# One of each head's sums of kept scores and negated maximum made by an accumulating DMA

## The chip, the cores and the metric

The kernel runs on one core of a Trainium2 chip. The core has TensorE (PE, with its weight loads as PEld), VectorE (DVE), ScalarE (ACT), GpSimd (POOL) and SyncE (SP). Each engine works through its own queue in the order in which the program was written, and waits at an instruction until the semaphores it names have come. Transfers run on 16 DMA engines that all queues share. The metric is the device time of one execution in microseconds (us). Three runs of the kernel before took 1121.7, 1123.69 and 1124.69 us; the median is 1123.69 us.

## The reference, cut to what matters

The input x has 2048 rows of 448 values in fp32. It is normalised, and one block of attention (16 heads of 28 columns that share one key and one value) and one gated MLP with 1792 hidden columns both read the result. Their sum with x is the output.

```
xn = layernorm(x)
q = (xn @ wq) as 16 heads of 28;  k = xn @ wk;  v = xn @ wv      # k and v shared by all heads
p = softmax(q @ k.T * 28 ** -0.5)                                 # exact maximum taken out per query row
att = (p @ v, heads side by side) @ wo
h = silu(xn @ w1) * (xn @ w3)
out = x + att + h @ w2
```

## The kernel before, in words

The 2048 query rows are cut into four chunks of 512. A head in the sense of the kernel is one of the 16 heads on one chunk, so there are 64, numbered 0 to 63. For each of them the 2048 keys are 16 tiles of 128. Scores stand transposed: a tile has 128 keys in its partitions and 512 queries along them.

Each head passes through two stages. In the first, `leads`, PE makes all 16 score tiles (`ld`, 16 matmuls of 512 columns) and DVE takes a running maximum of them (`mx`, L800 and L803). Ten or twelve of the 16 tiles are kept: ACT copies them from PSUM into SBUF (`pa`, L797), two tiles to a pair of 128 x 1024. The column maxima are folded, negated and stored in DRAM as one row of 512 values (`md`). Two transfers read that row back: one appends it to the queries (`qs`), one spreads it over 128 partitions (`mb`, 256 KB).

In the second stage, `weights_of`, a kept pair has the negated maximum added by POOL (L839: `pa` plus `mb`, 128 x 1024) and goes through the exponential in place on ACT (L841). The tiles that were not kept are computed again by PE with the maximum as an 85th row (`sc`, L846), and ACT takes their exponential from PSUM (`pb`, L849). In `values`, PE multiplies eight tiles by v (`av`, L866), four of this head and four of the head before it. Two heads that run at once fill the time between them: a head begins every half `T`.

The keeping plan is `TEN` (pairs that begin at tiles 2, 5, 8, 11, 14) or, for every second head from head 12, `TWELVE` (1, 4, 6, 9, 11, 14): 346 pairs in all. The last pair of a head in the order of the second stage is always the one that begins at tile 14.

Beside this the MLP runs as 56 steps (14 hidden tiles for each chunk): gate `g` and up `u` matmuls, tanh on ACT, two products on DVE, a high and a low part `h` on ACT and POOL (L698, L700), then the down products `dn`. In the first chunk, weights are read raw, split into a high and a low part by ACT and POOL (L650, L652, L666, L668) and stored in DRAM; later chunks load them from there.

The order of the work is made by a planner inside the kernel. Every instruction gets an engine, a cost and a due time. The planner then plays the machine through and lets each free engine take, of the work whose inputs are ready and whose buffers are free, the piece that is due first. Buffers are pages of 2 KB a partition and pairs of them; `MOST`, `SPARE`, `SOON` and `EARLY` limit who may hold how many. `PUT` shifts the due time of each kind of work. `T0`, `T`, `LEAD`, `SPAN`, `XDUE`, `MDUE` and the like set the due times of heads and of MLP steps, and `RATE`, `LATE` and `BACKLOG` describe transfers. So a change of a table reorders all five queues.

Of the kernel before, what the change touches and what calls it, by code (L numbers as in the profile page):

```python
# [13 lines left out]
ALU = mybir.AluOpType  # L14
# [6 lines left out]
P = 128  # L21
TC = 512
# [21 lines left out]
AVK = 4  # L44
T0, T, LEAD, SPAN = 73.28, 32.63, 14.04, 29.75
XDUE = (4.15, 8.15, 12.15, 16.15)
QDUE, QSTEP = 21.57, 6.09
SINGLE = 2
XSTORE = 22.5, 16.1
MDUE, MRUSH, MSTEP = 40, 11, 10.34  # L50
MEND = 7.58
RATE = 18.1
QUEUES = 16
LANES = 8
BACKLOG = 1565.91
LATE = 901.2
HLV = 0
EARLY = 16
BULK = ("w13", "w2", "x", "raw", "raw2", "acc")
SOON = {"pa": 30.2, "qs": 15.3, "acc": 15.9, "o": 18.3, "x": 24.2}  # L60

PUT = {"ACT ": -1.32, "ACT at pa": 0.93, "ACT at pb": -0.15, "ACT at x": 1.75, "ACT at xp": 8.68,
        "ACT av o": -9.5, "ACT h mi": -0.39, "ACT h t": -0.01, "ACT kv qp": -3.95, "ACT lb o oh": -0.08,
        "ACT mi t": -0.59, "ACT mi x": 2.0, "ACT o oh": 1.81, "ACT qp qt": -0.15, "ACT raw w13": -16.73,
        "ACT raw wo": 7.09, "DVE ": 1.37, "DVE acc": -5.45, "DVE acc xn": -2.36, "DVE at m": -0.89,
# [11 lines left out]
PAIRS = 39  # L77
PAGES = 96 - 2 * PAIRS
SLACK = 5.49
REST = 70.26  # L80
LOADING = 60
BANKS = 8
MOST = {"pa": 33, "x": 25, "acc": 10, "w13": 9, "w2": 8, "h": 3, "oh": 12, "wo": 4, "xt": 3, "xn": 1, "wq": 14,
        "qt": 4, "pb": 12, "raw": 4, "raw2": 5, "t": 2, "qs": 5, "m": 4, "mxt": 7, "mb": 7, "o": 19, "lb": 7,
        "xp": 33, "wr": 8, "kv": 7, "at": 5, "mi": 21, "av": 9, "qp": 14}
SPARE = {"x": 2, "acc": 4, "w13": 2, "w2": 4, "raw": 2, "raw2": 2, "qt": 6, "wo": 1, "qs": 2}

# [26 lines left out]
class Plan:  # L114
# [42 lines left out]
    def order(self):  # L157
# [8 lines left out]
        queues, landed = [0.0] * QUEUES, [0.0] * LANES  # L166
# [50 lines left out]
        now, todo = 0.0, len(self.ops)  # L217
        while todo:
            progress = True
            while progress:  # L220
                progress = False
                for e in self.ENGINES:
# [16 lines left out]
                    o = best  # L239
# [9 lines left out]
                    if o.port:  # L249
# [95 lines left out]
def build(ctx, tc, x, wq, wk, wv, wo, w1, w3, w2, out):  # L345
    nc = tc.nc
    plan = Plan()
# [21 lines left out]
    def fixed(ap):  # L369
        return Buf(None, "fixed", ap=ap)  # L370
# [11 lines left out]
    def gps(n, fn, **k):  # L382
        return plan.op("POOL", pool(n), fn, lat=pool_lat(n), **k)
# [67 lines left out]
    acc = {}  # L451
# [24 lines left out]
    for g, (lo, hi) in enumerate(QROWS):  # L476
        b = page("wr", f"wqr{g}")
# [22 lines left out]
    for qc in range(NQ):  # L500
# [3 lines left out]
        for t in range(TT):  # L504
            sbf = fixed(sts[t])
            b, m = x_in[qc][t], mvb[qc][t]
# [250 lines left out]
    stacks, pt, mbs, avb, og, ohl = {}, {}, {}, {}, {}, {}  # L757
    lead_first, av_last = {}, [None]
    md = {h: dr.tile([1, TC], F32, tag=f"md{h}", name=f"md{h}") for h in range(NH)}
# [3 lines left out]
    def kept(h):  # L763
        return TWELVE if h >= FROM and h % OF < MANY else TEN

    def begin(h):
# [12 lines left out]
    def leads(h):  # L779
# [51 lines left out]
    def weights_of(h, i):  # L831
# [5 lines left out]
        if kt in keeps:  # L837
            p, b = pt[h, kt][0], mbs[h]
            gps(1024, lambda: nc.gpsimd.tensor_add(p.ap, p.ap, b.ap.unsqueeze(1).broadcast_to([P, 2, TC])),  # L839
                reads=[b], writes=[p], prio=-3.0)  # L840
            act(1024, lambda: nc.scalar.activation(p.ap, p.ap, AF.Exp, scale=SCALE), psum=False, writes=[p],  # L841
# [175 lines left out]
```

## Time and profile before

| | value |
|---|---|
| three runs, us | 1121.7, 1123.69, 1124.69 |
| the profiled execution: span from first to last instruction, us | 1120.7 |
| what the runs lie above that span, us | 1.0 to 4.0, the median 3.0 |
| busy of the span: PE, POOL, ACT, DVE | 99%, 89%, 88%, 84% |
| 346 kept pairs on POOL, mean ns and sum | 2412 ns, 821.7 us |
| DMA: share of 16 engines, moved | 46.9%, 167.50 MB |

The profile's span runs from the first instruction to the last; the time of a run also holds what lies around them. Of the profiled execution the page has the span alone. Busy time of an engine says how much of the span it worked; the table of stretches says when. An engine that idles costs something only if another one, which sets the end, waits for it. A row of a wait names the waiting instruction first and then what released it.

### The profile page before, as it was taken

Reading aid. Unit: us, or ns where it says so; the run is one execution under the profiler, and the core shown is the slowest. Engines: PE = TensorE matmul, PEld = TensorE weight load, DVE = VectorE, ACT = ScalarE, POOL = GpSimd, SP = SyncE. Lnnn points to the kernel's source line nnn. Section 1 sums busy time; section 2 is a strip of 40 time slices with the busy share of each in tenths; the row PEclk is TensorE's granted clock in tenths of the full one; section 3 lists DMA queues with packets and bytes.
Section 4 is the critical chain, followed back from the end, with each engine's and each line's share of the span. In section 5 each row is a group of like instructions: output and inputs, shape, how many; then the busy total and the mean of one; then the engine's idle time right before and its main releaser. Section 6 shows DMA issues by size and latency. Waiting matters only on the chain.

```text
span 1120.7 us, 18422 instructions
## 1 busy us (share of the span) xinstructions
PE 1104.6 (99%) x5758; PEld 736.5 (66%) x5758; DVE 946.0 (84%) x1802; ACT 982.9 (88%) x1628; POOL 994.1 (89%) x499
## 2 busy tenths in 40 slices
PE   6999999999999999999999999999999999999998
PEld 4877667666666676666666666666666676667664
DVE  7879776898898989899899888899889889898834
ACT  3466888999999989999899999999899989998962
POOL 3226999999999998999999998999989999999983
PEclk9999999999999999999999999999999999999999
DMA  6887777576425246242631461514452534335410
GB/s 180 264 264 257 254 255 255 159 227 214 164 62 155 69 135 207 59 140 75 232 124 50 148 224 53 166 45 156 142 173 75 174 127 150 102 92 161 142 56 33
DMA packets 99017, 168.66 MB, mean 150 GB/s; under 512 B 19804, under 2 KB 61468, under 8 KB 98920
## 3 DMA queue, kind: packets, MB, share of 16 engines
q1 hardware_dynamic: 98920, 167.50, 46.9%
q8 instruction: 45, 0.74, 0.3%
q14 instruction: 52, 0.43, 0.1%
HBM read 126.94 MB, written 39.83 MB: 149 GB/s over the span
## 4 chain that ended last, share of the span: by engine, by line
PE 94%; DVE 2%; ACT 2%; DMA 1%; issue 0%; SPq 0%; DVEq 0%; ACTq 0%
PE ld L792 22%; PE av L866 21%; PE g L409 12%; PE u L409 12%; PE dn L409 11%; PE sc L846 8%; PE q L409 4%; PE wo L409 3%; PE xp L541 1%; DVE mx L803 1%; ACT pa L841 1%; ACT pa L797 1%; DVE acc L723 1%; DMA acc<-x 0%; DVE sums L939 0%
## 5 line engine op out<-in xcount | busy, mean ns | idle before, releaser
L839 POOL TENSOR_TENSOR pa<-pa,mb 128x1024 f32<-128x1024 f32 x346 | 821.7, 2412 | 9.0 <-DMA mb<-md 6.4
L803 DVE TENSOR_TENSOR mx<-ld,mx 128x512 f32<-128x512 f32 x896 | 581.9, 682 | 73.0 <-PE ld L792 49.1
L797 ACT ACTIVATE pa<-ld 128x512 f32<-128x512 f32 x692 | 400.8, 622 | 39.7 <-PE ld L792 30.3
L841 ACT ACTIVATE pa<-pa 128x1024 f32<-128x1024 f32 x346 | 373.9, 1088 | 14.8 <-POOL pa L839 14.3
L792 PE MATMUL ld<-qs,kst 84*128 84x512 f32 x1024 | 351.4, 405 | 0.4 <-DVE mx L803 0.2
L792 PEld LDWEIGHTS ld<-qs,kst 84*128 84x128 f32 x1024 | 189.9, 189 | 100.8 <-DVE mx L803 21.6
L866 PE MATMUL av<-pa,vst 128*32 128x512 f32 x1384 | 248.3, 599 | 0.0
L866 PE MATMUL av<-pb,vst 128*32 128x512 f32 x664 | 245.6, 597 | 0.0
L849 ACT ACTIVATE pb<-sc 128x512 f32<-128x512 f32 x332 | 202.6, 617 | 17.3 <-PE sc L846 16.5
L409 PE MATMUL dn<-w,h 128*128 128x448 f32 x672 | 156.7, 368 | 0.0
L409 PEld LDWEIGHTS dn<-w,h 128*128 128x128 f32 x672 | 125.6, 188 | 23.3 <-issue 3.0
L846 PE MATMUL sc<-qs,kst 85*128 85x512 f32 x332 | 134.7, 410 | 0.0
L866 PEld LDWEIGHTS av<-pa,vst 128*32 128x32 f32 x1384 | 51.6, 109 | 91.7 <-issue 82.9
L700 POOL TENSOR_TENSOR h<-t,h 128x512 fp32r<-128x512 f32 x56 | 72.7, 1299 | 41.9 <-ACT h L698 40.6
L846 PEld LDWEIGHTS sc<-qs,kst 85*128 85x128 f32 x332 | 62.6, 188 | 45.7 <-DVE mx L803 11.1
L652 POOL TENSOR_TENSOR w<-raw,w 128x512 fp32r<-128x512 f32 x28 | 36.2, 1302 | 42.7 <-ACT w L650 25.2
L866 PEld LDWEIGHTS av<-pb,vst 128*32 128x32 f32 x664 | 48.1, 109 | 33.2 <-issue 33.2
L723 DVE TENSOR_TENSOR acc<-dn,acc 128x448 f32<-128x448 f32 x80 | 49.4, 618 | 23.0 <-PE dn L409 21.9
L409 PE MATMUL g<-x_0m,w 128*128 128x512 f32 x168 | 58.1, 396 | 0.0
L409 PE MATMUL g<-x_2m,w 128*128 128x512 f32 x168 | 56.6, 396 | 0.0
L409 PE MATMUL u<-x_2m,w 128*128 128x512 f32 x168 | 54.9, 393 | 0.0
L409 PE MATMUL u<-x_0m,w 128*128 128x512 f32 x168 | 54.9, 395 | 0.0
(85 smaller groups left out, 1187.0 us busy)
## 6 DMA issues: line engine op xcount, KB each, us to landing
w<-w13s SPq DMA_DIRECT2D x84, 512.0 KB
w<-w2s SPq DMA_DIRECT2D x42, 448.0 KB
mb<-md SPq DMA_DIRECT2D x64, 256.0 KB
w13s<-w SPq DMA_DIRECT2D x28, 512.0 KB
qs<-qd SPq DMA_DIRECT2D x64, 112.0 KB
wo<-wos SPq DMA_DIRECT2D x16, 448.0 KB
w2s<-w SPq DMA_DIRECT2D x14, 448.0 KB
raw<-w SPq DMA_DIRECT2D x28, 192.0 KB
```

Source lines behind the costliest of these rows:

```text
L409: nc.tensor.matmul(dst.ap[0:n, 0:width], lv(lb), rv(rb), start=(i == 0), stop=(i == len(terms) - 1))
L652: gps(512, lambda: nc.gpsimd.tensor_sub(l.ap, r.ap, f32(h.ap)), reads=[r, h], writes=[l], prio=-6.0)
L700: sub(512, lambda: eng.tensor_sub(hl.ap, p.ap, f32(hh.ap)), reads=[p, hh], writes=[hl], prio=2 * half)
L723: vec(448, lambda: nc.vector.tensor_add(a.ap[:, 0:D], o.ap[:, 0:D], a.ap[:, 0:D]), reads=[o, a], prio=1.0))
L792: last = pe(512, lambda m=m, kt=kt: nc.tensor.matmul(m.ap, kst_ap[0:KS, kt * P:(kt + 1) * P], q.ap[0:KS], start=True, stop=True), reads=[q ...
L797: act(512, lambda m=m, p=p, i=int(kt not in keeps): nc.scalar.activation(p.ap[:, i], m.ap, AF.Copy), reads=[m], parts=[p])
L803: vec(512, lambda m=m: nc.vector.tensor_max(mx.ap, m.ap, mx.ap), reads=[m], writes=[mx])
L839: gps(1024, lambda: nc.gpsimd.tensor_add(p.ap, p.ap, b.ap.unsqueeze(1).broadcast_to([P, 2, TC])), reads=[b], writes=[p], prio=-3.0)
L841: act(1024, lambda: nc.scalar.activation(p.ap, p.ap, AF.Exp, scale=SCALE), psum=False, writes=[p], prio=-1.0, after=[sqrt_last])
L846: pe(512, lambda: nc.tensor.matmul(o.ap, kst_ap[0:KS + 1, kt * P:(kt + 1) * P], q.ap[0:KS + 1], start=True, stop=True), reads=[q, kst[kt / ...
L849: act(512, lambda: nc.scalar.activation(p.ap, o.ap, AF.Exp, scale=SCALE), reads=[o], writes=[p], prio=0.0, after=[sqrt_last])
L866: nc.tensor.matmul(a.ap[r:r + 32], vst_ap[:, kept(g)[2][n]], p.ap if i is None else p.ap[:, i], start=(n < 2), stop=(n >= KT - 2), skip_gr ...
```

## The change

For each head one kept pair, the one that begins at tile 14, no longer gets its negated maximum from POOL's add. POOL issues a DMA instead (L850 after the change) that reads the row `md` from DRAM, repeated for 128 partitions and both tiles, and adds it to the pair in SBUF. The other four or five pairs of the head are added by POOL as before (L854), with `mb`, which is still loaded. So 64 of the 346 adds become 64 DMAs, and the exponential of these pairs waits for the DMA. `BYDMA` is the number of such pairs per head, `ISSUE` the time in ns that the planner books on POOL for one, `AHEAD` the shift of its due time in us. The planner also learns that a transfer can come from POOL.

The DMA scratch in SBUF is set to 4096 bytes a partition, and the planner's buffers grow from 96 to 102 pages of 2 KB, three of which pairs more: 42 instead of 39. All tables of the planner are given new numbers.

```
-T0, T, LEAD, SPAN = 73.28, 32.63, 14.04, 29.75
+BYDMA, ISSUE, AHEAD = 1, 1000.0, -18.18
+T0, T, LEAD, SPAN = 71.07, 32.62, 14.04, 29.77
...
-MDUE, MRUSH, MSTEP = 40, 11, 10.34
-MEND = 7.58
+MDUE, MRUSH, MSTEP = 39.93, 11, 11.03
+MEND = 9.81
...
-PAIRS = 39
-PAGES = 96 - 2 * PAIRS
+PAIRS = 42
+PAGES = 102 - 2 * PAIRS
...
-                    if e == "SP":
+                    if o.size:
+                        begun = now if e == "SP" else now + o.cost
                         for j in range(o.k):
-                            queues[j] = max(queues[j], now) + o.size / o.k / RATE
+                            queues[j] = max(queues[j], begun) + o.size / o.k / RATE
...
+    def n_of(keeps, order, kt):
+
+        return [k for k in order if k in keeps].index(kt)
...
-        d = fixed(md[h])
+        d = mdb[h] = fixed(md[h])
...
         if kt in keeps:
             p, b = pt[h, kt][0], mbs[h]
-            gps(1024, lambda: nc.gpsimd.tensor_add(p.ap, p.ap, b.ap.unsqueeze(1).broadcast_to([P, 2, TC])),
-                reads=[b], writes=[p], prio=-3.0)
+            if n_of(keeps, order, kt) >= len(keeps) - BYDMA:
+                plan.op("POOL", ISSUE, lambda: nc.gpsimd.dma_start(
+                    p.ap, md[h].unsqueeze(1).broadcast_to([P, 2, TC]), accum_op=ALU.add),
+                    reads=[mdb[h]], writes=[p], prio=AHEAD, size=2 * 2 * P * TC * 4)
+            else:
+                gps(1024, lambda: nc.gpsimd.tensor_add(p.ap, p.ap, b.ap.unsqueeze(1).broadcast_to([P, 2, TC])),
+                    reads=[b], writes=[p], prio=-3.0)
             act(1024, lambda: nc.scalar.activation(p.ap, p.ap, AF.Exp, scale=SCALE), psum=False, writes=[p],
                 prio=-1.0, after=[sqrt_last])
...
-    nc = _bacc.Bacc("TRN2", target_bir_lowering=False, num_devices=1)
+    nc = _bacc.Bacc("TRN2", target_bir_lowering=False, num_devices=1, dynamic_dma_scratch_size=4096)
```

Three places show what the new order does. In the names, the number behind `pa`, `mb`, `md`, `ld`, `sc` or `pb` is the head, the next one the tile; the last number is the builder's. DMASW names the semaphores of DMAs that POOL issued, DMAHW those of SP's.

The first place is POOL's queue at head 6. Before, the pair of tile 14 is the head's last add, behind adds of head 7:

```order
L839 TENSOR_TENSOR pa6_8_2077<-pa6_8_2077,mb6_2456 128x1024
L839 TENSOR_TENSOR pa6_11_2191<-pa6_11_2191,mb6_2456 128x1024
L914 TENSOR_TENSOR o0_1949<-o0_1949,lb0_2645 128x512 [waits DMAHW4_49,DMAHW5_49,DMAHW3_49,DMAHW2_49]
L627 TENSOR_TENSOR wo_1_2677<-wor1_2607,wo_1_2677 128x448 [waits DMAHW1_49,DMAHW6_49,DMAHW0_49,DMAHW7_49,Activation_49,Pool_49]
L918 TENSOR_TENSOR oh0_2738<-o0_1949,oh0_2738 128x512 [waits PE_49,Activation_49]
L839 TENSOR_TENSOR pa7_2_2279<-pa7_2_2279,mb7_2671 128x1024 [waits DMAHW6_49]
L652 TENSOR_TENSOR w130_13_0_2732<-raw13_0_2594,w130_13_0_2732 128x512 [waits DMAHW0_49]
L652 TENSOR_TENSOR w130_13_1_2756<-raw13_1_2695,w130_13_1_2756 128x512 [waits DMAHW2_49,DMAHW1_49,DMAHW3_49,PE_49,Activation_49]
L839 TENSOR_TENSOR pa7_5_2296<-pa7_5_2296,mb7_2671 128x1024
L839 TENSOR_TENSOR pa6_14_2255<-pa6_14_2255,mb6_2456 128x1024
```

Now, at the same head:

```order
L854 TENSOR_TENSOR pa6_8_2038<-pa6_8_2038,mb6_2349 128x1024
L850 DMA pa6_14_2136<-md6_151 128x2x512
L854 TENSOR_TENSOR pa6_11_2093<-pa6_11_2093,mb6_2349 128x1024
L674 TENSOR_TENSOR w20_11_2589<-raw2_11_2521,w20_11_2589 128x448 [waits DMAHW3_49,PE_49,Activation_49]
L626 MEMSET wor3_2604 128x512 [waits Pool_49]
L706 TENSOR_TENSOR h11_2630<-t11_2545,h11_2630 128x512 [waits DMAHW2_49,Activation_49]
L850 DMA pa7_14_2438<-md7_152 128x2x512 [waits DMAHW6_49]
```

The DMA of tile 14 stands ahead of the head's own add of tile 11, and waits for nothing that has not been waited for already.

The second place is ACT's queue at the exponentials of the same pairs. Before, up to that of tile 14 of head 6:

```order
L849 ACTIVATE pb6_10_2833<-sc6_10_2832 128x512 [waits Activation_49]
L841 ACTIVATE pa7_5_2296<-pa7_5_2296 128x1024 [waits Pool_49]
L797 ACTIVATE pa10_5_2864<-ld10_5_2863 128x512 [waits PE_49]
L797 ACTIVATE pa10_5_2864<-ld10_6_2870 128x512 [waits PE_49]
L797 ACTIVATE pa9_14_2880<-ld9_14_2879 128x512 [waits DMAHW6_49,PE_49]
L841 ACTIVATE pa6_14_2255<-pa6_14_2255 128x1024 [waits Pool_49]
```

Now, from the exponential of tile 11, whose add is POOL's last work ahead, to that of tile 14:

```order
L856 ACTIVATE pa6_11_2093<-pa6_11_2093 128x1024 [waits Pool_49]
L807 ACTIVATE pa8_14_2609<-ld8_14_2608 128x512 [waits PE_49]
L864 ACTIVATE pb5_13_2613<-sc5_13_2612 128x512 [waits PE_49,Pool_49]
L704 ACTIVATE h11_2630<-t11_2545 128x512 [waits DMAHW2_49,DVE_49]
L807 ACTIVATE pa8_14_2609<-ld8_15_2617 128x512 [waits DVE_49]
L656 ACTIVATE w130_12_0_2651<-raw12_0_2533 128x512 [waits DMAHW5_49,DMAHW4_49,DMAHW1_49]
L631 ACTIVATE wo_1_2655<-wor1_2225 128x448 [waits DMAHW3_49,DMAHW2_49,DMAHW0_49]
L896 ACTIVATE o1_2665<-av2_2141 64x512 [waits PE_49]
L807 ACTIVATE pa9_2_2662<-ld9_2_2661 128x512 [waits PE_49]
L807 ACTIVATE pa9_5_2680<-ld9_5_2679 128x512 [waits PE_49]
L856 ACTIVATE pa6_14_2136<-pa6_14_2136 128x1024 [waits DMASW6_49]
```

The exponential of tile 14 waited for POOL and now waits for a DMA that POOL issued; ten instructions of ACT, the first one an exponential that needs an add of POOL behind that issue, stand ahead of it.

The third place is PE's queue at the end, from the last head's last values matmuls. Before:

```order
L866 MATMUL av31_12500<-pa63_14_12377,vst_76 32x512 [waits Activation_49]
L866 MATMUL av31_12500<-pa63_14_12377,vst_76 32x512
L866 MATMUL av31_12500<-pb63_10_12625,vst_76 32x512
L866 MATMUL av31_12500<-pb63_13_12640,vst_76 32x512
L409 MATMUL dn3_12_0_12709<-w23_12_12303,h54_12679 128x448 [waits DVE_49,Activation_49]
L409 MATMUL dn3_12_0_12709<-w23_12_12303,h54_12679 128x448
L409 MATMUL dn3_12_0_12709<-w23_12_12303,h54_12679 128x448 [waits Pool_49]
L409 MATMUL dn3_12_0_12709<-w23_13_12369,h55_12704 128x448 [waits DMAHW0_49,Activation_49]
L932 MATMUL sums_12714<-o15_12565,spread_70 128x512 [waits DVE_49]
L409 MATMUL dn3_12_0_12709<-w23_13_12369,h55_12704 128x448
L409 MATMUL dn3_12_0_12709<-w23_13_12369,h55_12704 128x448 [waits Pool_49]
L409 MATMUL dn3_12_1_12720<-w23_12_12303,h54_12679 128x448 x3
```

Now:

```order
L881 MATMUL av31_12475<-pa63_14_12359,vst_76 32x512 [waits Activation_49]
L881 MATMUL av31_12475<-pa63_14_12359,vst_76 32x512
L881 MATMUL av31_12475<-pb63_10_12645,vst_76 32x512
L881 MATMUL av31_12475<-pb63_13_12649,vst_76 32x512
L415 MATMUL u55_12686<-x3_4m_9351,w133_13_1_12289 128x512
L415 MATMUL u55_12686<-x3_6m_9363,w133_13_1_12289 128x512
L415 MATMUL u55_12686<-x3_0m_9300,w133_13_1_12289 128x512 x2
L415 MATMUL u55_12686<-x3_2m_9323,w133_13_1_12289 128x512 x2
L947 MATMUL sums_12706<-o15_12527,spread_70 128x512 [waits DVE_49]
L415 MATMUL dn3_12_0_12715<-w23_12_12265,h54_12677 128x448 x2
L415 MATMUL dn3_12_0_12715<-w23_12_12265,h54_12677 128x448 [waits Pool_49]
L415 MATMUL dn3_12_0_12715<-w23_13_12367,h55_12708 128x448 [waits DMAHW2_49,Activation_49]
```

Six matmuls of the last up product moved from ahead of the last values to behind them; in all 43 matmuls follow the last values, where there were 37.

More of the change, by code (lines that the diff above doesn't have):

```diff
@@ L54 @@
 LANES = 8
-BACKLOG = 1565.91
+BACKLOG = 1567
 LATE = 901.2
 HLV = 0
-EARLY = 16
+EARLY = 47
 BULK = ("w13", "w2", "x", "raw", "raw2", "acc")
[L60 to L65, printed above, removed]
[11 rows of a table removed]
-PAIRS = 39
-PAGES = 96 - 2 * PAIRS
+SOON = {"acc": 43.58, "wr": 41.58, "xt": 49.19, "xn": 48.49, "mi": 40.27, "x": 48.01, "wq": 51.79, "qp": 41.28,
[3 rows of a table added]
+PUT = {"ACT ": 12.12, "ACT at pa": 1.04, "ACT at pb": 0.34, "ACT at x": -14.78, "ACT at xp": 26.15,
+        "ACT av o": -36.65, "ACT h t": -8.3, "ACT kv qp": -42.54, "ACT mi t": -14.91, "ACT mi x": 38.09,
+        "ACT o oh": -30.4, "ACT pa": 0.72, "ACT qp qt": 8.28, "ACT raw w13": -3.85, "ACT raw wo": -0.79,
+        "ACT raw2 w2": -37.84, "ACT wq wr": -41.94, "DVE ": 3.54, "DVE acc": 1.48, "DVE acc mi": 11.24,
[6 rows of a table added]
+        "POOL mb pa": 0.57, "POOL o oh": -14.84, "POOL pa": 7.12, "POOL raw": 5.67, "POOL raw w13": -33.37,
[4 rows of a table added]
+PAIRS = 42
+PAGES = 102 - 2 * PAIRS
 SLACK = 5.49
@@ L82 @@
 BANKS = 8
[L83 to L86, printed above, removed]
+MOST = {"acc": 16, "wr": 4, "xt": 3, "xn": 1, "mi": 23, "x": 40, "wq": 12, "qp": 30, "qt": 4, "kv": 15, "at": 5,
+        "xp": 42, "raw": 20, "wo": 12, "w13": 9, "raw2": 14, "w2": 12, "t": 24, "h": 3, "qs": 5, "pa": 26,
+        "m": 9, "mxt": 20, "mb": 21, "pb": 9, "av": 37, "o": 29, "lb": 1, "oh": 12}
+SPARE = {"acc": 2, "wr": 8, "xn": 3, "x": 1, "wq": 7, "qt": 7, "raw": 1, "w13": 2, "raw2": 1, "w2": 3, "h": 2,
+        "qs": 2, "mxt": 1, "o": 3, "lb": 1, "oh": 1}
 class Buf:
@@ L757, in build @@
     stacks, pt, mbs, avb, og, ohl = {}, {}, {}, {}, {}, {}
-    lead_first, av_last = {}, [None]
+    lead_first, av_last, mdb = {}, [None], {}
     md = {h: dr.tile([1, TC], F32, tag=f"md{h}", name=f"md{h}") for h in range(NH)}
```

6 lines of the change are left out of this document (3 added, 3 removed), and 24 rows, old and new, of tables (PUT, SOON).

## The prediction

> **What bounds the kernel now.** I read the page's busy times first, then the table of stretches, the order of time on PE, the waits, the DMA queues, and last the end of the program.
>
> ```profile
> span 1120.7 us, 18422 instructions
> PE 1104.6 (99%) x5758; PEld 736.5 (66%) x5758; DVE 946.0 (84%) x1802; ACT 982.9 (88%) x1628; POOL 994.1 (89%) x499
> ...
> PE 94%; DVE 2%; ACT 2%; DMA 1%; issue 0%; SPq 0%; DVEq 0%; ACTq 0%
> ...
> L839 POOL TENSOR_TENSOR pa<-pa,mb 128x1024 f32<-128x1024 f32 x346 | 821.7, 2412 | 9.0 <-DMA mb<-md 6.4
> ...
> L797 ACT ACTIVATE pa<-ld 128x512 f32<-128x512 f32 x692 | 400.8, 622 | 39.7 <-PE ld L792 30.3
> L841 ACT ACTIVATE pa<-pa 128x1024 f32<-128x1024 f32 x346 | 373.9, 1088 | 14.8 <-POOL pa L839 14.3
> ```
>
> PE is busy for 1104.6 of 1120.7 us and is 94% of the chain that ended last. POOL, from which work is taken, is at 89%, ACT at 88%. The stretches say where PE's missing 16.1 us are:
>
> ```profile
> core 0: us, PE busy (x) PEld busy (x) DVE busy (x) ACT busy (x) POOL busy (x), PEclk, DMA share, GB/s
> 0.00:28.00 28.00, 17.75 (x75) 13.34 (x76) 21.22 (x53) 10.80 (x22) 9.52 (x14) 0.94 0.67 179
> 28.00:56.00 28.00, 28.00 (x141) 22.59 (x140) 24.02 (x55) 13.37 (x27) 6.11 (x5) 1.00 0.81 264
> 84.00:112.00 28.00, 27.78 (x123) 21.61 (x122) 26.04 (x48) 19.32 (x34) 18.40 (x12) 1.00 0.77 258
> 112.00:168.00 56.00, 56.00 (x282) 38.28 (x281) 42.42 (x78) 48.93 (x83) 56.00 (x32) 1.00 0.74 254
> 168.00:224.00 56.00, 56.00 (x291) 38.55 (x290) 42.05 (x79) 49.05 (x83) 55.69 (x35) 1.00 0.65 208
> 224.00:280.00 56.00, 56.00 (x297) 36.79 (x296) 49.97 (x97) 54.27 (x93) 55.78 (x31) 1.00 0.69 220
> 560.00:700.00 140.00, 140.00 (x751) 90.38 (x750) 126.12 (x241) 133.16 (x219) 132.56 (x62) 1.00 0.38 121
> 1064.00:1092.00 28.00, 28.00 (x155) 18.92 (x157) 11.46 (x22) 19.20 (x30) 24.91 (x13) 1.00 0.20 62
> 1092.00:1120.70 28.70, 23.22 (x109) 13.58 (x101) 11.82 (x20) 7.91 (x13) 10.15 (x9) 0.95 0.08 32
> ```
>
> 10.25 us lie in the first 28 us, before any kept score exists, and 5.48 us in the last 28.7 us. From 112 to 280 us POOL is full (167.47 of 168), and still PE is busy for all 168 us at a granted clock of 1.00: POOL keeps pace there and sets nothing.
>
> Busy could hide gaps, since a matmul's record is longer than the distance to the next. The order of time on PE settles it:
>
> ```profile
> 621.31 0.63 PE L409 MATMUL u<-x_0m,w 128*128 128x512 f32 x2
> 621.77 0.62 PE L409 MATMUL u<-x_2m,w 128*128 128x512 f32 x2
> 622.23 0.62 PE L409 MATMUL u<-x_4m,w 128*128 128x512 f32 x2
> 622.68 0.39 PE L409 MATMUL u<-x_6m,w 128*128 128x512 f32 x1
> ```
>
> Two matmuls every 0.46 us, 0.23 us for 512 columns, three times running. A gap would show as a longer step, and none does. The kernel is bound by PE's own work, and the change takes none of it away: the order has 4733 matmuls before and after (the page's 5758 records hold each values matmul twice), the same 346 kept pairs, the same 332 recomputed scores.
>
> The Trainium skill weighs against reading it so. Its page Trainium Kernel Development and Optimization (Performance Expectations) calls matmul busy time a bad measure and weight-load busy a good one; weight loads are at 66%, so by that rule PE has room and a lighter POOL could pay. The even steps of 0.23 us speak for the row, not for the rule.
>
> **The change, part by part.**
>
> ```profile
> ACT pa L841 <- POOL pa L839: 14.3, 19, 1.9
> ...
> L829 SPq DMA_DIRECT2D mb<-md x64: 319/343/730, 88.1 to 1070.0; - x64
> ...
> 86.05 3.64 DMA w13s<-w
> ...
> w13s<-w SPq DMA_DIRECT2D x28, 512.0 KB
> ...
> q1 hardware_dynamic: 98920, 167.50, 46.9%
> ```
>
> Removed on POOL: 64 of 346 adds at 2.412 us, 154.4 us. Added: 64 DMA issues. The trace has no DMA issued by POOL. Below lies SP's issue of the same row broadcast to half the length, 0.343 us (median); above, the add it replaces, 2.412 us. The form is nearest to SP's, with twice the rows, so I take 0.69 us: 44 us. POOL falls from 994 to about 884 us (79%). On the path this is worth nothing in the middle, since PE idles there for no one. What ends is part of the 14.3 us that ACT waited for POOL's adds in 19 places; ACT idles 138 us in all, so that is worth 0 us as well.
>
> Added on the DMA engines: each accumulate fetches 512 KB of broadcast row, reads 512 KB of scores and writes them back. 167.5 MB took 46.9% of 16 engines, so 512 KB takes 0.469 x 1120.7 x 0.524/167.5 = 1.64 us of all engines. One pass is the low end, three passes, 4.9 us, the high end; two, 3.3 us, is what I take, because the row read 128 times is the lightest of the three. That is 64 x 3.3 = 210 us, 19 points more share. In the middle (0.38 at 560 to 700 us) it fits easily. From 84 to 280 us it adds 3.3 us per 16.3 us of head, 0.20, to 0.65 to 0.77: close to full.
>
> Landing: the chain shows a 512 KB transfer in 3.64 us in a stage at 0.77 share. So from issue to landing 3.64 us for one pass; with a second pass 3.64 + 1.64 = 5.3 us, which I take; the high end is three times the row, 10.9 us.
>
> Added wait: ACT's exponential of tile 14 waits for this landing instead of POOL. Behind it in ACT's queue stand copies of lead scores, whose banks PE needs next. How much time the new order leaves I count from rows: POOL's work between the DMA and the last add that ACT consumes ahead of that exponential, at 2.41 us an add and 1.3 us for the other subtractions, plus ACT's work from there (0.62 us a copy or score, 1.09 us a kept pair). For head 6, whose rows stand with the change, that is one add and ten ACT instructions, 2.4 + 6.6 = 9 us. Over the 63 heads with such an add ahead the median is 11.4 us, the least 3.5 us, and two lie under 5.3 us, by 2.3 us together. ACT idles 138/64 = 2.15 us per head, so both vanish: 0 us. With 10.9 us, 27 of 63 would be late.
>
> The Trainium skill's page DMA: Bandwidth & Descriptors (Anatomy of one DMA) fits a GpSimd-issued DMA by 2.0 us plus bytes at 436 GB/s: an estimate of 3.2 us for one pass and 5.6 us for three. By the page two heads are late and the sum stays; by three times the row it does not. No row before shows an accumulate, so I keep the row's end for the range.
>
> On POOL the DMA waits for md, the negated maximum in DRAM; the adds queued behind it wait for mb, which is read from that same md later, so the wait costs POOL nothing new. SP loses and gains no DMA; its transfers share the engines, as counted above. The six more 2 KB pages remove no wait that PE shows: 0 us.
>
> The end is reordered. Before, from the last values matmul on:
>
> ```profile
> 1104.76 1.03 PE L866 MATMUL av<-pb,vst 128*32 128x512 f32 x4
> 1105.84 0.59 ACT L881 ACTIVATE o<-av 64x512 f32<-64x512 f32 x1 [0.49 <-PE av L866]
> 1106.46 0.69 DVE L882 TENSOR_TENSOR o<-av,o 64x512 f32<-64x512 f32 x1 [1.78 <-ACT o L881]
> 1107.21 1.12 PE L932 MATMUL sums<-o,spread 128*128 128x512 f32 x2 [0.41 <-DVE o L882]
> ...
> 1108.38 0.97 DVE L939 RECIPROCAL sums<-sums 128x128 f32<-128x128 f32 x1 [1.22 <-PE sums L932]
> ...
> 1114.01 1.01 PE L409 MATMUL wo<-wo,oh 128*128 128x448 f32 x3 [0.40 <-ACT oh L941]
> ...
> 1115.72 1.00 PE L409 MATMUL wo<-wo,oh 128*128 128x448 f32 x3 [0.70 <-ACT oh L941]
> ...
> 1117.22 0.62 DVE L723 TENSOR_TENSOR acc<-wo,acc 128x448 f32<-128x448 f32 x1
> ```
>
> After them PE has idles of 0.41, 0.40 and 0.70 us. Six u matmuls (6 x 0.23 = 1.4 us) now stand behind the last values and can fill those: at most -1.4 us. Against it, DVE does six adds of 0.62 us after the last normalising product where it did four, and two fewer before it: up to +0.5 us. I take -0.5 us. The first 35 rows on PE are the same matmuls with the same waits, so the 8 to 10 us of the start stay.
>
> Sum: 1120.7 + 0 (POOL) + 0 (DMA, landing) - 0.5 = 1120.2 us of span. The median of the runs, 1123.69, lies 3.0 us above this execution's span; with that, **1123.2 us**.
>
> **The rivals.** (1) Faster: the retuned order packs start and end better than I count, or PE has room that its busy time hides. For: 15.7 us of idle at both ends. Against: at most a third of it is within reach, 4 to 6 us, giving 1118 to 1120. It decides from -3.4 us on. (2) Slower by late landing: at 9 us from issue to landing ten heads are late by 26.5 us together, 7.5 us of it beyond ACT's 2.15 us per head; PE follows in order, so +7.5 to +26 us, 1131 to 1150. It decides at about 8 us (9 heads, 3.4 us beyond ACT's idle time). For: two queues now share the engines. Against: the median room of 11.4 us. (3) Slower by crowding at 84 to 280 us: about 12 accumulates x 3.3 us = 40 us (59 at three passes) against (1 - 0.70) x 196 = 59 us free. If weights are asked for just in time, 0.5 to 1.7 us of each delay reach PE: +6 to +20 us, 1129 to 1143. (4) POOL's issue is dear: from (1120.7 - 994)/64 + 2.41 = 4.4 us an issue POOL is the bound; at 6 us it works 994 - 154 + 384 = 1224 us, so 1230. (5) PE meets many small new waits in the other order: +4 to +10 us, 1128 to 1134. That the DMA does nothing is no rival: the order shows all 64.
>
> **How the numbers follow.** 0.3%, 3.4 us, is about what a measurement can tell (the three runs span 1121.7 to 1124.69). No change as summed: 0.42, its own range 1120.3 to 1126.6. (1) 0.16. (2) 0.15. (3) 0.15. (4) 0.04. (5) 0.08. So faster 0.16, same 0.42, slower 0.42. The range 1118.5 to 1143 leaves out (4), the upper half of (2) and the lower end of (1), 0.04 + 0.07 + 0.06 = 0.17.
>
> **What would show it.** Right: PE busy still near 1104.6 us with its idle at both ends, POOL near 884 us, DMA share near 66%, 282 adds left, and no wait of ACT's kept exponential on a DMA above 1 us on average. Wrong: a large row of that exponential waiting for a DMA (2), PE behind w or x loads between 84 and 280 us (3), an issue on POOL above 4.4 us (4), or PE idle spread over the middle behind DVE and ACT (5).

## The result and the profile after

The changed kernel takes 1125.99 us, the median of 13 runs (1123.59 to 1129.01), against 1123.69 us of the kernel before in the same session. The ratio is 1.0025, with a 95% interval of 1.0015 to 1.0034: slower by about 2.5 us (2.3 by the medians). Measured twice more, it came to 1.0014 (1.0005 to 1.0023) and 1.0013 (0.9987 to 1.0039; wide, because two of the 18 runs before took 1130.4 and 1132.5 us; by the medians 3.3 us). So the loss is about 0.2%, and two of the three intervals exclude no change. The profiled execution took 1125.03 us, 2.7 us above its span.

The page of the kernel after: the lines that answer to those shown of before, then the new line and the landing of its transfer.

```profile
span 1122.3 us, 18448 instructions
...
PE 1104.7 (98%) x5758; PEld 735.3 (66%) x5758; DVE 952.9 (85%) x1802; ACT 980.5 (87%) x1628; POOL 919.8 (82%) x499
...
q1 hardware_dynamic: 98920, 167.50, 46.4%
q0 software_dynamic: 17408, 33.56, 18.7%
...
L854 POOL TENSOR_TENSOR pa<-pa,mb 128x1024 f32<-128x1024 f32 x282 | 695.2, 2594 | 21.1 <-DMA mb<-md 15.7
...
L856 ACT ACTIVATE pa<-pa 128x1024 f32<-128x1024 f32 x346 | 369.1, 1086 | 15.3 <-POOL pa L854 14.9
...
L850 POOL DMA_DIRECT2D pa<-md x64 | 87.0, 1359 | 11.1 <-ACT pa L807 5.0
...
pa<-md POOLq DMA_DIRECT2D x64, 512.0 KB, 7.5
```

POOL fell by 74 us, the DMA engines took on 18.7 points, the 64 accumulates land 7.5 us after their issue, and the exponential of the kept tiles (L856) waits for POOL's adds as before (14.9 us, before 14.3) and for no DMA. PE's busy time is unchanged, and the span is 1.6 us longer.

The table of stretches shows where PE stands idle that did not before. Kernel before, then after:

```profile
core 0: us, PE busy (x) PEld busy (x) DVE busy (x) ACT busy (x) POOL busy (x), PEclk, DMA share, GB/s
0.00:56.00 56.00, 45.75 (x214) 35.93 (x215) 45.23 (x107) 24.17 (x48) 15.63 (x19) 0.97 0.74 222
...
224.00:336.00 112.00, 111.92 (x592) 73.66 (x591) 99.60 (x189) 107.45 (x181) 110.91 (x56) 1.00 0.52 167
336.00:1064.00 728.00, 728.00 (x3883) 474.23 (x3882) 646.53 (x1229) 689.06 (x1130) 694.90 (x323) 1.00 0.41 130
```

```profile
core 0: us, PE busy (x) PEld busy (x) DVE busy (x) ACT busy (x) POOL busy (x), PEclk, DMA share, GB/s
0.00:56.00 56.00, 45.26 (x218) 35.53 (x219) 46.81 (x110) 26.84 (x52) 15.83 (x19) 1.00 0.76 223
56.00:112.00 56.00, 56.00 (x247) 43.03 (x245) 47.06 (x87) 36.85 (x64) 29.44 (x19) 1.00 0.83 263
112.00:224.00 112.00, 111.70 (x577) 76.39 (x576) 87.30 (x160) 98.52 (x168) 105.67 (x69) 1.00 0.81 232
224.00:336.00 112.00, 110.32 (x569) 70.89 (x572) 97.85 (x181) 103.72 (x174) 95.44 (x53) 1.00 0.82 236
336.00:1064.00 728.00, 728.00 (x3881) 476.10 (x3883) 649.94 (x1227) 684.98 (x1128) 637.52 (x321) 1.00 0.61 163
```

From 224 to 336 us PE idles 1.68 us where it idled 0.08, in the stretch where the DMA share rose from 0.52 to 0.82. From 336 to 1064 us nothing changed for PE, though the share rose there too (0.41 to 0.61). The first row carries a trap: the granted clock is 0.97 before and 1.00 after, so the profiled execution after had a better start by chance (below).

One of the waits stands in the chain of the kernel after, around 260 us:

```profile
253.65 0.70 DVE o L897
...
254.37 3.35 DMA l<-o
...
257.79 6.70 DMA lc<-l
...
264.51 0.04 DVE lc L921
...
264.68 0.64 DVE mx L813
...
265.37 0.73 PE ld L802 x2
```

The 8 KB of softmax sums were stored in 3.35 us (l) and took 6.70 us to come back from DRAM (lc). VectorE, which works in order, waited for them, then freed the PSUM bank that PE wanted. That made the first suspect: the accumulates crowd the DMA engines, and a small transfer lands late.

A finer measure than busy time: I take each step from one matmul's start to the next, subtract the usual step of its kind (0.23 us for 512 columns, 0.20 for 448, 0.52 from a values matmul to one of another kind; steps into a values matmul are left out), and sum the excesses over 0.03 us. In us, by slices of the span, over both profiles of the kernel before, the three of after, and one of the experiments (e5, below):

```
slice (us)    before  again | after  again  third | e5
0-56            7.43   7.68 |  6.47   6.48   7.73 | 7.77
  without the half-clock steps of the start (0.2 us each)
                6.2    6.3  |  6.5    6.5    6.1  | 6.2
56-112          1.51   1.53 |  0.49   0.49   0.69 | 0.69
112-224         1.26   1.27 |  1.95   1.95   2.03 | 2.03
224-280         0.93   0.92 |  2.86   1.95   1.82 | 1.93
280-336         1.08   1.09 |  3.12   4.17   4.45 | 2.55
336-1064       10.7   10.7  | 10.4   10.5   10.6  | 10.7
1064-end        3.46   3.46 |  2.33   2.34   2.33 | 2.33
sum, corrected 25.2   25.2  | 27.7   27.9   28.1  | 26.4
```

With the start put right, after is 2.5 to 2.9 us longer in every pair of profiles, which is the size of the measured loss. All of it lies between 112 and 336 us; the stretch 56-112 and the end gave back 0.8 to 1.0 and 1.1 us.

### The profile page after: what moved, and what is told of

The parts are those of the page before. It is cut to its first block, busy times and chain, and to the rows that moved or that the text cites. A ratio compares the mean times of both kernels' runs of the same rounds, so it can differ in the third digit from the quotient of the medians.

```text
span 1122.3 us, 18448 instructions
## 1 busy us (share of the span) xinstructions
PE 1104.7 (98%) x5758; PEld 735.3 (66%) x5758; DVE 952.9 (85%) x1802; ACT 980.5 (87%) x1628; POOL 919.8 (82%) x499
## 3 DMA queue, kind: packets, MB, share of 16 engines
q1 hardware_dynamic: 98920, 167.50, 46.4%
q0 software_dynamic: 17408, 33.56, 18.7%
## 4 chain that ended last, share of the span: by engine, by line
PE 94%; DVE 2%; DMA 1%; ACT 1%; issue 1%; SPq 0%; ACTq 0%; DVEq 0%
PE ld L802 22%; PE av L881 21%; PE u L415 13%; PE g L415 12%; PE dn L415 12%; PE sc L861 7%; PE q L415 3%; PE wo L415 3%; DMA lc<-l 1%; PE xp L547 1%; DVE mx L813 0%; DMA acc<-x 0%; DVE acc L729 0%; DVE sums L954 0%; ACT pa L807 0%
## 5 line engine op out<-in xcount | busy, mean ns | idle before, releaser
L854 POOL TENSOR_TENSOR pa<-pa,mb 128x1024 f32<-128x1024 f32 x282 | 695.2, 2594 | 21.1 <-DMA mb<-md 15.7
L813 DVE TENSOR_TENSOR mx<-ld,mx 128x512 f32<-128x512 f32 x896 | 590.1, 684 | 63.5 <-PE ld L802 30.2
L856 ACT ACTIVATE pa<-pa 128x1024 f32<-128x1024 f32 x346 | 369.1, 1086 | 15.3 <-POOL pa L854 14.9
L415 PE MATMUL dn<-w,h 128*128 128x448 f32 x672 | 166.2, 368 | 0.1
L706 POOL TENSOR_TENSOR h<-t,h 128x512 fp32r<-128x512 f32 x56 | 76.0, 1357 | 94.6 <-ACT h L704 90.8
L850 POOL DMA_DIRECT2D pa<-md x64 | 87.0, 1359 | 11.1 <-ACT pa L807 5.0
L658 POOL TENSOR_TENSOR w<-raw,w 128x512 fp32r<-128x512 f32 x28 | 38.9, 1418 | 37.4 <-ACT w L656 30.5
L729 DVE TENSOR_TENSOR acc<-dn,acc 128x448 f32<-128x448 f32 x80 | 49.2, 616 | 19.4 <-PE dn L415 18.7
```

Of the source, the lines that this page charges most:

```text
L415: nc.tensor.matmul(dst.ap[0:n, 0:width], lv(lb), rv(rb), start=(i == 0), stop=(i == len(terms) - 1))
L706: sub(512, lambda: eng.tensor_sub(hl.ap, p.ap, f32(hh.ap)), reads=[p, hh], writes=[hl], prio=2 * half)
L729: vec(448, lambda: nc.vector.tensor_add(a.ap[:, 0:D], o.ap[:, 0:D], a.ap[:, 0:D]), reads=[o, a], prio=1.0))
L813: vec(512, lambda m=m: nc.vector.tensor_max(mx.ap, m.ap, mx.ap), reads=[m], writes=[mx])
L850: plan.op("POOL", ISSUE, lambda: nc.gpsimd.dma_start(p.ap, md[h].unsqueeze(1).broadcast_to([P, 2, TC]), accum_op=ALU.add), reads=[mdb[h]], ...
```

## The experiments

Two theories. T1: the accumulates' traffic costs the time. T2: the retuned order of all instructions costs it, whatever is transferred. A third, T3, stands in the expectation of e1: the issues slow POOL, and PE waits for it. Most runs keep the order of the kernel after to the last instruction and change the size of one thing, so that two traces can be laid over each other matmul by matmul.

**e1: the accumulates on one partition.**

```
-   p.ap, md[h].unsqueeze(1).broadcast_to([P, 2, TC]), accum_op=ALU.add),
+   p.ap[0:1], md[h].unsqueeze(1).broadcast_to([1, 2, TC]), accum_op=ALU.add),
```

> The kernel after with every instruction at its place in every queue, but each accumulating transfer covers one partition of the tile instead of 128 (so 127 of its rows go without the maximum: that part of the computation is left out). T1, the accumulates' traffic costs the time (it crowds the DMA engines, small transfers such as the softmax sums lc land late, VectorE waits in its queue, PSUM banks come free late): q0's 18.7 % of the DMA time goes nearly to 0, the lc transfer at about 258 us takes about 3 us instead of 6.70, the PE gaps of the slices 224-336 us fall from 6.0 us to about 2, and the time falls by 3 to 5 us against the kernel after, to 0.998-1.000 of the kernel before. T2, the new order costs the time by itself (VectorE's chain of maxima packed between maxima of scores at 284-291 us, waits of PE): the time stays within 1 us of the kernel after, 1.002-1.003 of the kernel before. T3, GpSimd is slowed by the issues (87.0 us of issues, adds of 2.59 instead of 2.41 us) and PE waits for it: the issue of one row is near 0.5 us, POOL falls by 40 us or more, and the time falls as under T1, but without a change in lc.

1124.52 us against 1122.82, ratio 1.0017 (1.0008 to 1.0026). The page:

```profile
q0 software_dynamic: 2048, 0.27, 0.3%
...
L854 POOL TENSOR_TENSOR pa<-pa,mb 128x1024 f32<-128x1024 f32 x282 | 682.0, 2490 | 22.2 <-DMA mb<-md 20.7
...
L850 POOL DMA_DIRECT2D pa<-md x64 | 54.6, 854 | 13.6 <-PE dn L415 5.0
```

18.4 of 18.7 points of DMA time are gone, POOL is 27 us lighter, lc is not waited for, and the loss stays. By the ratios the time is 0.9 us under the kernel after; it lies just below T2's range (1.002 to 1.003), and its interval excludes T1's (0.998 to 1.000). T3 is tested less sharply, because an issue still takes 0.85 us of POOL; against it stands that the waits of PE, below, are for VectorE and not for POOL.

**e2: the new tables without the transfer.**

```
-BYDMA, ISSUE, AHEAD = 1, 1000.0, -18.18
+BYDMA, ISSUE, AHEAD = 0, 1000.0, -18.18
```

> The kernel after with BYDMA = 0: no accumulating transfer, all 346 sums by GpSimd adds, the new tables, the three more pairs of buffers and the 4 KB scratch kept; the planner, which now sees 64 more adds, writes its own order. T1 (traffic): within 0.1 % of the kernel before or faster, 0.996-1.001. T2 (tables): 1.002 or more of the kernel before. The new tables were not made for this program, so a slow result alone does not prove T2; a result at 1.000 or less speaks against T2.

1129.49 us, ratio 1.0061 (1.0046 to 1.0076). **e3: the transfer with the old tables** (everything from T0 to SPARE as in the kernel before, 39 pairs, 18 pages; the rest as after).

> The reverse: the tables, pairs and pages of the kernel before (39 pairs, 18 pages) with the accumulating transfer and its early issue and the 4 KB scratch. T1: the traffic costs here too, 1.002-1.005 of the kernel before, with lc transfers over 5 us and PE gaps in 224-336 us of 5 us or more. T2: within 0.1 % of the kernel before. A much slower time (over 1.006) would say that the old tables do not suit the moved instructions, and decides nothing.

1144.18 us, ratio 1.0199 (1.0174 to 1.0223). Each half of the change alone is worse than both together: each set of tables was made for one program, and in these two others that the planner ordered by them PE meets new stalls (by the sums above, corrected for the start, about 34 us in e2 and 45 in e3 against 27.7). By the bounds set ahead, e2 falls on T2's side, with the reserve stated there, and e3 decides nothing.

**e4: no wait for lc.**

```
-   vec(16, lambda: nc.vector.reciprocal(lct, lct), writes=[lc], prio=4.0, cost=160.0)
+   vec(16, lambda: nc.vector.reciprocal(lcx, lcx), writes=[lc], prio=4.0, cost=160.0)
```

(lcx is a tile of ones, and the store of the reciprocals reads it too.)

> The kernel after with its order, except that VectorE's reciprocal of the softmax sums works on a tile of ones of its own and so does not wait for the transfer lc, which still runs (the division by the sums is left out). T1 in its narrow form, the late lc holds VectorE's queue: the wait of 0.82 us at 264.5 us and the PE gap of about 1.1 us there go, and the time falls by 1 to 2 us against the kernel after. Rival, other waits of the traffic or the order carry the loss: the time falls by less than 0.5 us.

1125.30 us, ratio 1.0019 (1.0009 to 1.0029). Laid over the trace of after, PE gains 0.9 us at 265 us, just where the wait was, but the time does not follow. The next runs say why.

**e5: one partition for heads 8 to 19 alone**, whose accumulates are issued between 246 and 405 us (not 330, as the expectation has it; the first six of the twelve go out by 318 us).

```
-   p.ap, md[h].unsqueeze(1).broadcast_to([P, 2, TC]), accum_op=ALU.add),
+   p.ap[0:rows(h)], md[h].unsqueeze(1).broadcast_to([rows(h), 2, TC]), accum_op=ALU.add),
+   rows = lambda h: 1 if 8 <= h <= 19 else P
```

> The kernel after with its order; the accumulates of heads 8 to 19 alone (issued between about 245 and 330 us) cover one partition instead of 128 (their other rows go without the maximum: that part is left out), the other 52 are whole. Theory A, the traffic costs only where it meets the weight transfers of 245-330 us: matmul for matmul PE gains 1.3 to 1.7 us on the kernel after between 254 and 328 us, as in the run with one row everywhere, and nothing after that, so the time equals that run's, 1.0015-1.002 of the kernel before. Rival B, the traffic costs a little everywhere: the gain is under 0.5 us.

1124.55 us, ratio 1.0014 (1.0005 to 1.0022). Between 254 and 328 us PE gains 1.53 us on the first profile of after, exactly as much as in e1. By the expectation that was theory A confirmed. It would have been written down so, had the control not come.

**e9: the kernel after again, unchanged.** (No edit.)

> The kernel after unchanged, profiled a second time. It is the control of the matmul-for-matmul comparison: if the gains of 0.9, 0.23, 0.24 and 0.14 us at 265, 289, 316 and 326 us belong to the removed traffic, two profiles of the same kernel differ there by under 0.1 us each, and differ only in the first 25 us (0 to 12 matmuls of the first head of the program at 0.43 instead of 0.23 us, 0 to 2.6 us) and in chance dips of the granted clock. If such steps come and go between two profiles of the same kernel, the traffic is not shown to be their cause.

1124.77 us, ratio 1.0014 (1.0005 to 1.0023). Start of the same matmul against the first profile of after, in us; all of these have the same order:

```
matmul at (us)   after again  third |   e1     e5     e4     e8    e10
37.1                 +0.02   +1.70  | +1.77  +1.42  +2.05  +0.66  +0.70
264.1                +0.05   +1.66  | +1.76  +1.39  +2.05  +0.62  +0.70
267.4                -0.87   +0.74  | +0.85  +0.48  +1.12  +0.24  -0.20
289.0                -0.88   +0.89  | +0.83  +0.46  +1.43  +0.23  -0.23
296.5                +0.52   +2.57  | +0.61  +0.24  +1.55  +1.55  +1.05
327.7                +0.15   +2.22  | +0.24  -0.13  +1.49  +1.00  +0.48
last                 +0.15   +2.39  | +0.33  +0.20  +1.70  +0.93  +0.60
```

The unchanged kernel shows the step of -0.9 us at 265 us too, and -0.31 us at 316 us. The late lc belongs to one execution and not to the kernel: VectorE waited for it 0.8 us in the first profile, and not at all in the second and third. In the first, the slow piece was the store ahead of it: lc was issued 3.4 us behind the store (257.79 after 254.37 us), in the second profile 1.8 us (256.25 after 254.41) and in the third 1.9 us. So e4 and e5 had compared themselves with one unlucky execution. What the step shows is that lc can be late while the accumulates run (0.8 and, in e8, 0.4 us, where lc itself took some 8.4 us; in two of four profiles with whole accumulates and the wait in place; never in the three with one row there, e1, e5 and e10). That is too few to give the traffic a price; by the times (e1 and e5 against after) it is none that can be measured.

The same control brought another difference, +1.40 us between 289 and 296 us. The stretches of this second profile of after:

```profile
290.00:292.00 2.00, 1.84 (x5) 1.21 (x6) 1.81 (x6) 2.00 (x6) 2.00 (x2) 0.67 1.00 394
292.00:294.00 2.00, 2.00 (x7) 1.78 (x6) 1.78 (x3) 1.83 (x3) 2.00 (x3) 0.50 0.65 146
294.00:296.00 2.00, 2.00 (x12) 1.86 (x10) 1.45 (x3) 1.06 (x1) 2.00 (x3) 0.97 1.25 368
```

and of the first:

```profile
290.00:292.00 2.00, 1.76 (x5) 0.80 (x5) 1.87 (x6) 2.00 (x4) 2.00 (x2) 1.00 1.02 390
292.00:294.00 2.00, 2.00 (x10) 1.87 (x11) 1.79 (x4) 2.00 (x4) 2.00 (x2) 1.00 0.80 243
```

The granted clock (the column behind POOL's) fell to 0.50 for some 3 us in the second, and some eight matmuls ran at half pace. It fell right behind three waits of PE: 0.32, 0.48 and 0.31 us at 288.1, 289.5 and 290.5 us, each for VectorE's running maximum (L813), which frees the bank that PE writes next. The first profile has the same waits (0.30, 0.27, 0.45 and 0.29 us from 289.0 to 291.4 us), and no dip.

The kernel before keeps PE busy there at the same DMA share, and e1, without the traffic, has the waits too. Before, then e1:

```profile
290.00:292.00 2.00, 2.00 (x11) 1.40 (x8) 1.93 (x3) 1.70 (x4) 2.00 (x2) 1.00 1.00 389
```

```profile
290.00:292.00 2.00, 1.71 (x5) 0.67 (x4) 1.88 (x6) 2.00 (x4) 2.00 (x2) 1.00 0.99 292
```

The chain of the first profile of after says what VectorE does meanwhile. Between the maxima that PE waits for (mx) stand steps of the fold of finished maxima (nm) and the add that joins two halves (o):

```profile
287.83 0.69 DVE mx L813
...
288.54 0.18 DVE nm L824
...
288.74 0.69 DVE mx L813
...
289.54 0.70 DVE o L897
...
290.27 0.70 DVE mx L813
...
291.01 0.89 PE sc L861 x2
```

**e6: POOL's relief alone**, in the order of the kernel before.

```
-   gps(1024, lambda: nc.gpsimd.tensor_add(p.ap, p.ap, b.ap.unsqueeze(1).broadcast_to([P, 2, TC])),
+   n = 8 if kt == [k for k in kept(h)[2] if k in keeps][-1] else TC
+   gps(1024, lambda: nc.gpsimd.tensor_add(p.ap[:, :, 0:n], p.ap[:, :, 0:n],
+                                          b.ap[:, 0:n].unsqueeze(1).broadcast_to([P, 2, n])),
```

> The kernel before with its order; the last add of each head's five or six covers 8 of 512 columns of each half (the rest goes without the maximum: that part is left out), and there is no accumulate. This is the taking away of 64 adds alone: POOL falls by 64 x about 2.2 = 140 us. By the prediction's step that GpSimd's relief is worth 0: the time is within 0.1 % of the kernel before. Rival, GpSimd's relief shortens the wait of the exponentials (15.1 us of idle on ACT behind L854 adds) and of PE behind it: 0.996-0.998.

1123.37 us against 1123.23, ratio 1.0000 (0.9991 to 1.0009). Its page:

```profile
PE 1103.4 (99%) x5758; PEld 735.6 (66%) x5758; DVE 946.0 (84%) x1802; ACT 981.8 (88%) x1628; POOL 857.2 (77%) x499
...
L842 ACT ACTIVATE pa<-pa 128x1024 f32<-128x1024 f32 x346 | 373.3, 1089 | 5.4 <-POOL pa L840 5.2
```

137 us off POOL and two thirds of ACT's wait for it gone, and nothing gained. What the change takes away is worth nothing in the old order.

**e7: the transfer at the place of the add**, in the order of the kernel before.

```
-   gps(1024, lambda: nc.gpsimd.tensor_add(p.ap, p.ap, b.ap.unsqueeze(1).broadcast_to([P, 2, TC])),
+   last = kt == [k for k in kept(h)[2] if k in keeps][-1]
+   gps(1024, lambda: nc.gpsimd.dma_start(p.ap, md[h].unsqueeze(1).broadcast_to([P, 2, TC]), accum_op=ALU.add)
+       if last else nc.gpsimd.tensor_add(p.ap, p.ap, b.ap.unsqueeze(1).broadcast_to([P, 2, TC])),
```

> The kernel before with its order; the last add of each head is an accumulating transfer issued at the place of the add, without the early issue and the new tables. An add holds its tile for 2.4 us, the transfer for an issue of about 1.4 and a landing of about 7.5 us, so the exponential behind it can run 6.5 us later. Theory that the early issue (18.18 us of due time) is needed: ACT waits for the transfer in most heads, 2 to 5 us each, and the time rises by 3 % or more. Rival, the buffers in flight cover it: under 0.5 %.

1249.84 us, ratio 1.1131 (1.1116 to 1.1146). The waits:

```profile
ACT pa L843 <- DMA pa<-md: 137.0, 39, 8.9
```

39 of 64 exponentials wait, 3.5 us on average, and PE behind them. In the kernel after and in e3, both with the early issue, no exponential waits for the transfer. So the early issue is what hides a landing of 7 us, with the old tables too; but with those it costs 2% elsewhere (e3), and the new tables bring that down to 0.2%.

**e8: a thinner add of the pair's halves.**

```
-   vec(512, lambda: nc.vector.tensor_add(o.ap[r], a.ap[64:128], o.ap[r])
+   vec(512, lambda: nc.vector.tensor_add(o.ap[r, 0:16], a.ap[64:128, 0:16], o.ap[r, 0:16])
```

> The kernel after with its order; VectorE's add that joins the two halves of a pair of heads (line 897, 0.69 us each) covers 16 of 512 columns (the rest of o is left out). Theory, in the new order VectorE's packed stretch at the end of a pair (fold of the maxima, this add, maxima of scores) is what PE waits for at 254-262 and 285-292 us: matmul for matmul PE gains 0.8 to 1.5 us there. Rival, the waits come from the transfers or from ACT: under 0.3 us.

1123.98 us, ratio 1.0013 (1.0004 to 1.0022). The gaps of PE at 261.3 and 261.8 us (0.27 and 0.36 us) are unchanged, and those at 289 to 291 us are 0.31, 0.26 and 0.63, together 1.2 us against 1.3 in the first profile of after. So this add is not what PE mainly waits for; the steps of the fold beside it were not tried.

**e10: e5 and e8 together.**

> The kernel after with its order, the accumulates of heads 8 to 19 on one partition (their other rows go without the maximum) and line 897's add on 16 of 512 columns (the rest of o is left out): the two removals together. Theory that transfers landing late and VectorE's packed stretches are the two causes of the loss: matmul for matmul PE gains 1.5 (traffic) + 0.3 to 0.8 us (line 897) on the kernel after between 254 and 328 us, and the time comes to 0.9995-1.001 of the kernel before. Rival, the rest of the loss lies elsewhere in the order: 1.0015 or more.

1123.57 us against 1123.18, ratio 1.0003 (0.9995 to 1.0012). The time is the lowest of the new order, but its trace does not explain it: the gaps at 261 and at 289 to 291 us stand there as before, and the clock dips behind them. The profiled execution, 1124.53 us, was the second slowest of the 11. Its interval overlaps that of e9, and its upper end, 1.0012 or 1.3 us, just takes in the calmest case below. I take it as unsettled.

**e11: the kernel before against itself, profiled again.** (No edit.)

> The kernel before, measured against itself and profiled again: the null of the comparison. Expected 0.9992-1.0008. Theory that the loss of the kernel after is in stalls of PE closely following each other, behind which the granted clock sometimes falls to 0.5 for about 3 us (window 290-300 us at 0.83 in three of seven profiles of the new order): the old order has no such stalls between 60 and 1060 us, so its profile has no 10 us window between 30 and 1090 us under 0.98 and its span differs from the first (1120.7 us) only by the head of the program, by -1.3 to +1.5 us. Rival, the dips come by chance at any place: the old order shows them too.

Ratio 1.0000 (0.9991 to 1.0009). The span is 1120.9 us, no stretch of 10 us between 30 and 1090 us has a clock under 0.98, and from the fortieth matmul to the last the trace stays 0.07 to 0.25 us behind the first.

**e12: the kernel after a third time.**

> The kernel after, profiled a third time, on the same chip as the null. By the theory it is 1.0010-1.0025 of the kernel before; the gaps of PE at 112, 261-263 and 289-291 us are there again with the same sizes (0.55, 0.27 + 0.37 and about 1 us), a dip of the clock stands at 291-296 us or nowhere, and the wait of VectorE for lc at 264 us lies between 0 and 0.9 us. Rival, the loss is chance of the runs: 1.0005 or less, or gaps elsewhere.

1126.47 us, ratio 1.0013 (0.9987 to 1.0039). The gaps are back with the same sizes: 0.55 us at 113.9, 0.27 and 0.36 at 262, and 0.41, 0.49 and 0.34 at 290 to 292 us, with a dip of the clock behind them (0.83 over 290 to 300 us). lc isn't waited for.

So T2 stands, and T1 falls as the main cause: with the traffic gone (e1), loss and waits stay. The new order has a wait of PE at 112 us and clusters of short waits at 262 and 290 us, in each of its eight profiles; the two profiles of the old order have one wait of 0.26 us between 100 and 1060 us. By slices the new waits cost 0.8 + 1.0 + 1.5 us, against 0.8 and 1.1 us won at 56-112 us and at the end: 1.2 to 1.4 us in the calmest case (e5). On top come accidents: the clock behind the cluster at 290 us (four of eight profiles, 1.3 to 1.7 us each) and the late lc. Which number of the new tables makes the clusters stays open: each change of one reorders the whole program, as e2 and e3 show. No run beat the kernel before.

## Why the prediction was right or wrong

The time, 1125.99 us, lies inside the likeliest case's own range (1120.3 to 1126.6), 2.8 us above the point; the direction is the other one: slower by 0.13 to 0.25%, with two of three intervals clear of no change, where no change was the likeliest. That it still lies in the range is in part luck: the missing term below is small against a range of 6 us, and the end and the stretch 56-112 us gave back 2 us, of which the sum had only 0.5.

- **What bounds the kernel: right.** PE's own work: 1104.6 us before, 1104.7 after, and e6 shows that a lighter POOL is worth 0.
- **POOL to about 884 us: it is 919.8.** The issue takes 1.36 us, not 0.69 (64 x 0.67 = 43 us; in the range of 0.343 to 2.412), which covers the 36 us by which POOL lies above the forecast. The records of the adds that stay are longer too, 2.59 us on average where they were 2.41, and up to 3.77; but they overlap their neighbours. Together the 282 cover 695.2 us, 2.47 us each, against 2.37 (821.7 / 346) before, so whether an add itself became slower is not shown. The relief is two thirds of what I took, and the worth was 0 anyhow (e6).
- **DMA engines +19 points: right** (18.7). An accumulate costs what two passes would, 3.3 us of all engines: 33.56 MB on q0 took 18.7 points, where 167.50 MB on q1 took 46.4. Whether two passes are the reason is not shown; it was a choice between one and three.
- **Landing 5.3 us: it is 7.5**, inside the range, and nearly at the 8 us from which rival (2) decides. The room counted from the order held: the exponential waits for no DMA. e7 shows what stood behind it: without that room, +127 us.
- **The Trainium skill's page DMA: Bandwidth & Descriptors (Anatomy of one DMA)** gave an estimate of 3.2 to 5.6 us for the landing; the measured 7.5 us is above both, and 7.0 us in e7, where the engines are less loaded (58% against 65% of the span on both queues), is too.
- **Rival (3), crowding at 84 to 280 us: near the place, wrong cause.** Two of the three places with new waits, 112 and 262 us, lie in that stretch, the costliest, 290 us, behind it. PE waited for no weight there. A small transfer came late in some executions; the whole traffic is worth less than can be measured (e1: 1.0017, after 1.0025, 1.0014, 1.0013).
- **The end, -0.5 us: it is -1.1.** The six u matmuls that moved there can fill more than I allowed; the bound was -1.4.
- **The step that failed** is the sum, "0 (POOL) + 0 (DMA, landing) - 0.5". It has terms for the start, the end and the two moved operations, and none for the 224 us between 112 and 336 us in which the retuned order puts the same instructions differently. I had that only as rival (5), "PE meets many small new waits in the other order", at 0.08 and +4 to +10 us. The mechanism was this rival's; its size is 3.2 us of new waits, less 2.0 won elsewhere, plus, in half of the profiles, 1.3 to 1.7 us behind a dip of the clock.
- The even steps of 0.23 us at 621 us, from which I judged the middle, were right for 336 to 1064 us (10.7 and 10.5 us of excess). The stretch where the weights are still being prepared, 112 to 336 us, needed a look of its own.

## What to carry to other kernels

When a change comes with a new order, the order itself is a term of the sum, even where the bound engine is at 99%: here it won 2.0 us in two places and lost 3.2 in three. Compare the waits of that engine slice by slice, not only where operations moved. Before a step of a microsecond in one trace is given to a cause, profile the unchanged kernel again: here the control showed the same step, and a clean theory fell. And what is taken from an engine that sets nothing is worth nothing (137 us off POOL: 1.0000), while its replacement may bring a latency (the issue and landing, 7.5 us, in place of an add of 2.4) that the program has to be arranged for.

## What the runs showed of the hardware

The start runs at half pace for a while, and how long differs between executions of one program. The first 24 projections in a row, in the kernel before, in after, and in e1, whose order is that of after:

```profile
15.65 7.37 PE L409 MATMUL q<-x,wq 128*126 128x512 f32 x24 [0.96 <-DVE x L551]
```

```profile
16.26 5.83 PE L415 MATMUL q<-x,wq 128*126 128x512 f32 x24 [0.96 <-DVE x L557]
```

```profile
15.33 8.50 PE L415 MATMUL q<-x,wq 128*126 128x512 f32 x24 [0.66 <-DVE x L557]
```

Their steps are 0.43 us at first and 0.23 us later; the number of slow steps was 6 and 7 in the two profiles before, and 0, 0, 8, 12, 8, 12, 7 and 5 in the eight of the new order: up to 2.5 us of the span by chance, as much as the effect under study. The Trainium skill's page TensorE: Matmul & The Clock Gate (Part 1: The HAM clock gate) says this: the activity window of about 3.4 us runs freely, so one kernel shows different numbers of cold matmuls. The traces agree that the number differs, 0 to 12 here.

The dip behind the waits at 290 us came without a long idle. The table in that section of the Trainium skill's page has the clock fall after an idle window of about 3.4 us, which is not the only case that the page has. Here it fell to 0.50 though no single wait was above 0.7 us and PE was busy for most of the 3 us before (1.84 of 2.00 us in the first row shown for the second profile). The waits come to some 1.1 to 1.5 us within 3 us in all eight profiles; behind them the clock fell in four, and each dip cost 1.3 to 1.7 us, as much as the waits themselves. That the waits trigger the dip rests on its place, which was the same in all four, and on other orders: in e2 two of three clusters (225 and 620 us) have a dip behind them, in e3 one at 201 to 204 us, and the kernel before (two profiles) and e6, without clusters, have none between 30 and 1060 us. It wasn't tried by taking the waits away, and what decides between dip and no dip stays open.

An accumulating transfer of 512 KB issued from GpSimd took 1.36 us of GpSimd to issue (0.85 us with one partition), 7.5 us from issue to landing (median; 6.0 to 11.2), and 18.7% x 1122.3 / 64 = 3.3 us of all 16 DMA engines. A transfer of 8 KB from DRAM to SBUF took 6.70 us in one execution and some 8.4 in e8, next to accumulates and weights.
